# Attention scores of a one-token decode step: from one row per head to keys on the partitions, with the softmax divided out after the value product

## The chip, the cores and the metric

The kernel runs on one core of a Trainium2 chip. A core has a matrix engine (TensorE, PE in the profile, with its weight loads shown as PEld), a vector engine (VectorE, DVE), an activation engine (ScalarE, ACT), a general engine (GpSimd, POOL) and a queue engine (SyncE, SP) which here issues all transfers. The engines run side by side and wait for each other by semaphores. TensorE reads on-chip memory (SBUF) and writes the accumulator memory (PSUM), of which there are eight banks of 128 partitions by 512 fp32 values. The metric is the device time in microseconds; lower is better.

## The reference

One token of width 640 goes through an attention block and a feed-forward block, each behind a layer norm without weights and with a residual. Cut to what matters:

```python
q = (layernorm(x) @ wq)                   # 32 heads of 128
k = k_cache[:, :, 4096 - 1024:, :]        # the last 1024 of 4096 keys, 32 heads
v = v_cache[:, :, 4096 - 1024:, :]
p = softmax(q @ k^T * 128**-0.5)          # per head: 1024 scores
h = x + (p @ v) @ wo                      # wo: 4096 x 640
out = h + (gelu(layernorm(h) @ w_gate) * (layernorm(h) @ w_up)) @ w_down   # inner width 1728
```

All inputs are bf16. Every weight and every used key and value is read once, 33.9 MB together.

## The kernel before

The program is one list of instructions for each engine, written out by hand; the order in each list is the order of execution. `Wt(engine, tokens)` makes an engine wait for what `M(engine, token, instruction)` has marked. There is no planner.

SP issues the transfers in the order in which they are needed (L203 to L228): x, five slices of wq, keys in eight groups of four heads, values in eight groups, wo in four quarters of eight heads, then w_gate, w_up and w_down in four pieces. wo lies over wq and so waits for the last use of wq (token "ps_q", L214); the feed-forward weights lie over the keys and wait for the last key transpose (L218).

TensorE works as follows.

- q (L277 to L282): 160 matmuls with one moving column each give q with its 128 dimensions on the partitions and one column for each head.
- Keys (L283 to L288): for each head, `pe_transpose_batch` (L245) turns eight 128x128 blocks of keys into one PSUM bank; there are four such banks in rotation. VectorE (20 heads) or ScalarE (12 heads) copies the bank to one of six slots of `kT_sb` (`evac_batch`, L349). Two heads later `pe_scores_batch` (L256) computes the scores. The stationary operand is a 128x32 block of `qmask` in which only the column of this head is filled, the moving operand the transposed keys, 512 at a time. Over 32 heads these matmuls accumulate into `psS`, 32 partitions (heads) by 1024 keys, in two banks.
- Softmax (L289 to L296, L382 to L393, L443 to L447): VectorE takes the maximum of each row of `psS` and makes a bias of it; ScalarE does one exponential over 32x1024 with the row sum; VectorE inverts the sum and puts it on a diagonal `diag_r`. Eight matmuls against this diagonal turn the probabilities to keys-on-partitions and divide by the sum in one go, and VectorE copies them to `e_sb`.
- Values (L298 to L304): 256 matmuls with one moving column, eight for each head, accumulate the head's output into a column of `ps_o`, which ScalarE copies to `oT_sb` (L449).
- Output projection (L309 to L315): for each head two matmuls, 512 and 128 wide, with the head's column as stationary operand.
- The second layer norm (L394 to L408, L450 to L453), then gate (L326), up (L333) and the elementwise GELU, and down (L340): 14 chunks of two matmuls, 512 and 128 wide.
- VectorE adds the residual and SP stores the row (L225 to L228).

The scale that ScalarE applies in the exponential (`scl`, L375) holds both 128**-0.5 and the first layer norm's inverse deviation, which is therefore not applied to q.

## Time and profile before

| | us |
|---|---|
| median of 6 runs | 101.83 (101.08 to 103.22) |
| the profiled execution, device time | 101.67 |
| its span, first to last instruction | 99.6 |
| TensorE matmuls busy | 71.7 (72%) |
| TensorE weight loads busy | 44.1 (44%) |
| VectorE busy | 23.4 (24%) |
| ScalarE busy | 20.5 (21%) |
| GpSimd busy | 2.3 (2%) |
| transfers, mean rate over the span | 341 GB/s, 33.9 MB |

In the profile the span is cut into 40 equal slices of 2.49 us; each digit is a busy share in tenths, where 9 is 90% or more. A row of the groups names the line, the engine, what is written and read, the shapes and the number of instructions, then busy time in total, mean ns of one, and the idle time before them with its cause. Matmuls overlap, so the mean of one is longer than the distance between two starts. The chain of waits is followed back from the last instruction: each piece is what released the next one. "issue" is time in which an engine waited for nothing that the profile shows. In the table of stretches a row has the stretch, its length, busy time and count of each engine, and at the end TensorE's granted clock as a share of full speed, the transfer share and GB/s.

### The profile page before, as it was taken

Reading aid. Unit: us, or ns where it says so; the run is one execution under the profiler, and the core shown is the slowest. Engines: PE = TensorE matmul, PEld = TensorE weight load, DVE = VectorE, ACT = ScalarE, POOL = GpSimd, SP = SyncE. Lnnn points to the kernel's source line nnn. Section 1 sums busy time; section 2 is a strip of 40 time slices with the busy share of each in tenths; the row PEclk is TensorE's granted clock in tenths of the full one; section 3 lists DMA queues with packets and bytes.
Section 4 is the critical chain, followed back from the end, with each engine's and each line's share of the span. In section 5 each row is a group of like instructions: output and inputs, shape, how many; then the busy total and the mean of one; then the engine's idle time right before and its main releaser. Section 6 shows DMA issues by size and latency. Waiting matters only on the chain.

```text
span 99.6 us, 2145 instructions
## 1 busy us (share of the span) xinstructions
PE 71.7 (72%) x990; PEld 44.1 (44%) x990; DVE 23.4 (24%) x52; ACT 20.5 (21%) x26; POOL 2.3 (2%) x12
## 2 busy tenths in 40 slices
PE   0110005999999999999999607990899971698990
PEld 0010005993554554455455106990444530694430
DVE  0500000053325533432552241000000028032003
ACT  5600000004351244435124464000000004200000
POOL 7100000000000000000000000000000000000000
PEclk9999999999999999999999998555559999655589
DMA  1899999999999999999999999999999999993000
GB/s 43 352 421 421 428 414 392 387 385 388 386 386 387 387 386 388 391 379 387 388 387 385 385 376 363 364 367 356 362 385 410 404 403 389 367 353 116 0 0 1
DMA packets 16443, 34.02 MB, mean 342 GB/s; under 512 B 498, under 2 KB 6324, under 8 KB 15796
## 3 DMA queue, kind: packets, MB, share of 16 engines
q1 hardware_dynamic: 16436, 33.90, 91.7%
q8 instruction: 7, 0.11, 0.5%
HBM read 33.90 MB, written 0.00 MB: 341 GB/s over the span
## 4 chain that ended last, share of the span: by engine, by line
PE 70%; DMA 13%; DVE 5%; ACT 4%; issue 3%; SPq 2%; DVEq 0%
PE psbank L253 19%; DMA wq_sb<-in_A_wq_dram 13%; PE psS L260 10%; PE psbank L311 9%; PE psbank L302 7%; PE psS L262 7%; PE psbank L343 5%; PE psS L280 4%; SPq L198 2%; PE psbank L313 2%; PE psbank L336 2%; PE psbank L329 2%; ACT E_sb L444 1%; ACT L453 1%; DVE mrow L383 1%
## 5 line engine op out<-in xcount | busy, mean ns | idle before, releaser
L253 PEld LDWEIGHTS psbank<-ident,K_sb 128*128 128x128 bf16 x256 | 15.5, 102 | 12.7 <-issue 12.7
L253 PE MATMUL psbank<-ident,K_sb 128*128 128x128 bf16 x256 | 20.7, 229 | 0.0
L358 ACT ACTIVATE kT_sb<-psbank 128x1024 bf16<-128x1024 bf16 x12 | 12.3, 1023 | 38.4 <-PE psbank L253 38.4
L356 DVE COPY kT_sb<-psbank 128x1024 bf16<-128x1024 bf16 x20 | 13.8, 692 | 20.0 <-PE psbank L253 20.0
L260 PE MATMUL psS<-kT_sb,qmask 128*32 128x512 bf16 x32 | 12.7, 396 | 0.1
L262 PE MATMUL psS<-kT_sb,qmask 128*32 128x512 bf16 x32 | 12.4, 387 | 0.0
L280 PE MATMUL psS<-xcT,wq_sb 128*128 128x1 bf16 x160 | 5.0, 166 | 9.7 <-DMA wq_sb<-in_A_wq_dram 9.7
L311 PE MATMUL psbank<-wq_sb,oT_sb 128*1 128x512 bf16 x32 | 11.0, 445 | 0.3 <-ACT oT_sb L449 0.3
L280 PEld LDWEIGHTS psS<-xcT,wq_sb 128*128 128x128 bf16 x160 | 4.7, 104 | 10.1 <-DMA wq_sb<-in_A_wq_dram 9.5
L302 PE MATMUL psbank<-e_sb,V_sb 128*128 128x1 bf16 x256 | 7.1, 165 | 2.8 <-issue 2.3
L302 PEld LDWEIGHTS psbank<-e_sb,V_sb 128*128 128x128 bf16 x256 | 6.9, 103 | 3.0 <-issue 2.3
L313 PE MATMUL psbank<-wq_sb,oT_sb 128*1 128x128 bf16 x32 | 7.7, 242 | 0.0
L343 PE MATMUL psbank<-K_sb,aT 128*1 128x512 bf16 (+1 forms) x14 | 6.3, 534 | 0.4 <-DVE aT L426 0.4
L311 PEld LDWEIGHTS psbank<-wq_sb,oT_sb 128*1 128x1 bf16 x32 | 3.0, 94 | 5.9 <-issue 2.6
L395 DVE TENSOR_TENSOR h_rowf<-psbank,x_row 1x512 f32<-1x512 f32 x1 | 0.7, 679 | 20.8 <-PE psbank L313 20.8
L260 PEld LDWEIGHTS psS<-kT_sb,qmask 128*32 128x32 bf16 x32 | 3.0, 93 | 4.0 <-ACT kT_sb L358 0.6
L345 PE MATMUL psbank<-K_sb,aT 128*1 128x128 bf16 (+1 forms) x14 | 3.8, 271 | 0.0
L378 DVE CAST qmask<-psS 128x32 bf16<-128x32 f32 x1 | 0.3, 301 | 14.6 <-PE psS L280 14.6
L343 PEld LDWEIGHTS psbank<-K_sb,aT 128*1 128x1 bf16 (+1 forms) x14 | 1.5, 107 | 3.9 <-issue 3.0
L262 PEld LDWEIGHTS psS<-kT_sb,qmask 128*32 128x32 bf16 x32 | 3.1, 96 | 0.1
L270 PE MATMUL psS<-ones_bf,xc_row 1*128 1x1 bf16 x5 | 0.3, 160 | 3.9 <-DVE psbank L371 3.9
L313 PEld LDWEIGHTS psbank<-wq_sb,oT_sb 128*1 128x1 bf16 x32 | 3.0, 94 | 0.0
(70 smaller groups left out, 33.2 us busy)
## 6 DMA issues: line engine op xcount, KB each, us to landing
K_sb<-in_A_k_cache_dram SPq DMA_DIRECT2D x8, 1024.0 KB, 15.8
V_sb<-in_A_v_cache_dram SPq DMA_DIRECT2D x8, 1024.0 KB, 14.3
wq_sb<-in_A_wq_dram SPq DMA_DIRECT2D x5, 1024.0 KB, 8.9
wq_sb<-in_A_wo_dram SPq DMA_DIRECT2D x4, 1280.0 KB, 14.9
K_sb<-in_B_w_gate_dram SPq DMA_DIRECT2D x1, 2160.0 KB, 16.3
K_sb<-in_B_w_up_dram SPq DMA_DIRECT2D x1, 2160.0 KB, 17.7
K_sb<-in_B_w_down_dram SPq DMA_DIRECT2D x2, 640.0 KB, 14.5
K_sb<-in_B_w_down_dram SPq DMA_DIRECT2D x1, 800.0 KB, 17.7
```

The source lines that it names most:

```text
L198: sp.dma_start(out=out_ap, in_=in_ap).then_inc(sem, 16)
L253: t = pe.transpose(psT[bank][:, kk * 128:(kk + 1) * 128], K_sb[:, h, kk, :], ident[:, :])
L260: pe.matmul(psS0, lhsT=qmask[:, h * H:(h + 1) * H], rhs=kT_sb[:, slot, 0:512], start=(h == 0), stop=(h == H - 1))
L262: t = pe.matmul(psS1, lhsT=qmask[:, h * H:(h + 1) * H], rhs=kT_sb[:, slot, 512:1024], start=(h == 0), stop=(h == H - 1))
L280: t = pe.matmul(ps_q[:, h:h + 1], lhsT=wq_sb[:, c, h * DH:(h + 1) * DH], rhs=xcT[:, c:c + 1], start=(c == 0), stop=(c == DC - 1))
L302: t = pe.matmul(ps_o[:, h:h + 1], lhsT=V_sb[:, h, kk, :], rhs=e_sb[:, col:col + 1], start=(kk == 0), stop=(kk == KK - 1))
L311: pe.matmul(psA0, lhsT=oT_sb[:, h:h + 1], rhs=wo_view[:, h, 0:512], start=(h == 0), stop=(h == H - 1))
L313: t = pe.matmul(psA1, lhsT=oT_sb[:, h:h + 1], rhs=wo_view[:, h, 512:D], start=(h == 0), stop=(h == H - 1))
L343: pe.matmul(psD0, lhsT=aT[0:m, fc:fc + 1], rhs=wd_view[0:m, fc, 0:512], start=(fc == 0), stop=(fc == FC - 1))
L345: t = pe.matmul(psD1, lhsT=aT[0:m, fc:fc + 1], rhs=wd_view[0:m, fc, 512:D], start=(fc == 0), stop=(fc == FC - 1))
L356: ins = eng.tensor_copy(out=kT_sb[:, slot, :], in_=psT[bank][:, :])
L358: ins = eng.activation(out=kT_sb[:, slot, :], in_=psT[bank][:, :], func=ACT.Copy)
```

## The change

The scores are computed with the roles of the operands exchanged. For each head, eight matmuls have a 128x128 block of the transposed keys as stationary operand and the head's q, one column of the new `qT_sb`, as the moving one. Each writes one column of `ps_s`: 128 keys on the partitions, 256 columns for 32 heads by eight blocks. Nothing accumulates over heads, and `qmask` with its fill is gone. ScalarE, not VectorE, copies q from PSUM, ahead of its first key copy.

The softmax is then done in this layout. VectorE takes the maximum of each head over its eight columns (128x32), TensorE transposes that (`psM`), VectorE takes the maximum over the 128 partitions, puts it on a diagonal, and a matmul with ones spreads it to all partitions (`psMB`). VectorE copies it, subtracts it from the scores, and ScalarE does one exponential over 128x256, which gives the operand of the value product directly. A matmul with ones sums over the partitions (`psE`, 128x256); VectorE sums the eight columns of each head and inverts. This last is not needed before the end of the value product: its result is multiplied by the inverse when it leaves PSUM, on VectorE in place of ScalarE's copy.

The number of TensorE matmuls for the scores goes from 64 to 256; the eight matmuls against the diagonal go, and three single ones come.

```diff
@@ layout of PSUM
-        psS0 = psS[0:H, 0:512]
-        psS1 = psS[0:H, 512:1024]
-        psE = psb[0][:, 0:KK * H]
+        SOFF = 64
+        MBOFF = 64
+        ps5 = psS[:, 512:1024]
+        ps_s = ps4[:, SOFF:SOFF + H * KK]
+        ps_s3 = ps_s.rearrange("p (h kk) -> p h kk", kk=KK)
+        psM = ps5.bitcast(BF16)[0:H, 0:128]
+        psE = ps5[:, 0:H * KK]
+        psMB = psb[6][:, MBOFF:MBOFF + H]
@@ prog_pool
-            pool.memset(qmask[:, :], 0.0)
@@ pe_scores_batch
-            Wt("pe", ("E", b), "qmask")
-            pe.matmul(psS0, lhsT=qmask[:, h * H:(h + 1) * H], rhs=kT_sb[:, slot, 0:512],
-                      start=(h == 0), stop=(h == H - 1))
-            t = pe.matmul(psS1, lhsT=qmask[:, h * H:(h + 1) * H], rhs=kT_sb[:, slot, 512:1024],
-                          start=(h == 0), stop=(h == H - 1))
+            Wt("pe", ("E", b), "qT")
+            t = None
+            for kk in range(KK):
+                col = h * KK + kk
+                t = pe.matmul(ps_s[:, col:col + 1], lhsT=kT_sb[:, slot, kk * 128:(kk + 1) * 128],
+                              rhs=qT_sb[:, h:h + 1], start=True, stop=True)
@@ prog_pe
-            M("pe", "ps_r1", pe.matmul(ps_r1[0:H, :], lhsT=ones_f[0:1, 0:H], rhs=mv[0:1, 3:4],
+            M("pe", "ps_r1", pe.matmul(ps_r1[:, :], lhsT=ones_f[0:1, 0:128], rhs=mv[0:1, 3:4],
...
-            Wt("pe", "E", "diag_r", ("E", n_batches - NB))
-            for bb in range(n_batches - NB, n_batches):
-                if bb % NB == 0:
-                    Wt("pe", ("E", bb))
-            for kk in range(KK):
-                t = pe.matmul(psE[:, kk * H:(kk + 1) * H], lhsT=E_sb[0:H, kk * 128:(kk + 1) * 128],
-                              rhs=diag_r[0:H, 0:H], start=True, stop=True)
-            M("pe", "psE", t)
-            Wt("pe", "e_sb")
+            Wt("pe", "m1")
+            M("pe", "psM", pe.transpose(psM, m1_bf[:, :], ident[:, :]))
+            Wt("pe", "diag")
+            M("pe", "psMB", pe.matmul(psMB, lhsT=ones_bf[0:H, 0:128], rhs=diag[0:H, 0:H],
+                                         start=True, stop=True))
+            Wt("pe", "e", "m2")
+            M("pe", "psE", pe.matmul(psE, lhsT=ones_bf[:, :], rhs=e_bf[:, :], start=True, stop=True))
+            Wt("pe", "mbs")
             for h in range(H):
                 Wt("pe", ("V", h // 4))
                 for kk in range(KK):
-                    col = kk * H + h
-                    t = pe.matmul(ps_o[:, h:h + 1], lhsT=V_sb[:, h, kk, :], rhs=e_sb[:, col:col + 1],
+                    col = h * KK + kk
+                    t = pe.matmul(ps_o[:, h:h + 1], lhsT=V_sb[:, h, kk, :], rhs=e_bf[:, col:col + 1],
                                   start=(kk == 0), stop=(kk == KK - 1))
@@ prog_dve
-            Wt("dve", "ps_q")
-            M("dve", "qmask", dve.tensor_copy(out=qmask_diag, in_=ps_q))
...
             Wt("dve", ("S", n_batches - 1))
-            M("dve", "mrow", dve.tensor_reduce(out=mrow[0:H, :], in_=psS[0:H, :], axis=AX.X, op=ALU.max))
-            Wt("dve", "mrow", "scl")
-            M("dve", "nb", dve.scalar_tensor_tensor(out=nb[0:H, :], in0=mrow[0:H, :], scalar=-1.0, in1=scl[0:H, :],
-                                                    op0=ALU.mult, op1=ALU.mult))
-            Wt("dve", "E")
-            M("dve", "rinv", dve.reciprocal(out=rinv[0:H, :], in_=se[0:H, :]))
-            Wt("dve", "rinv", "ident")
-            M("dve", "diag_r", dve.tensor_scalar(out=diag_r[0:H, 0:H], in0=ident[0:H, 0:H],
-                                                 scalar1=rinv[0:H, 0:1], scalar2=None, op0=ALU.mult))
+            M("dve", "m1", dve.tensor_reduce(out=m1_bf[:, :], in_=ps_s3, axis=AX.X, op=ALU.max))
+            Wt("dve", "psM")
+            M("dve", "m2", dve.tensor_reduce(out=m2[0:H, 0:1], in_=psM, axis=AX.X, op=ALU.max))
+            Wt("dve", "m2", "ident")
+            M("dve", "diag", dve.tensor_scalar(out=diag[0:H, 0:H], in0=ident[0:H, 0:H],
+                                               scalar1=m2[0:H, 0:1], scalar2=None, op0=ALU.mult))
+            Wt("dve", "psMB")
+            M("dve", "mbs", dve.tensor_copy(out=mbs[:, :], in_=psMB))
+            Wt("dve", "mbs")
+            mb3 = bass.AP(tensor=mbs[:, :].tensor, offset=mbs[:, :].offset,
+                          ap=[list(mbs[:, :].ap[0]), [1, H], [0, KK]])
+            M("dve", "sm", dve.tensor_tensor(out=sm[:, :].rearrange("p (h kk) -> p h kk", kk=KK),
+                                             in0=ps_s3, in1=mb3, op=ALU.subtract))
             Wt("dve", "psE")
-            M("dve", "e_sb", dve.tensor_copy(out=e_sb[:, :], in_=psE))
+            M("dve", "rs", dve.tensor_reduce(out=rs[:, :], in_=psE.rearrange("p (h kk) -> p h kk", kk=KK),
+                                             axis=AX.X, op=ALU.add))
+            Wt("dve", "rs")
+            M("dve", "rinv", dve.reciprocal(out=rinv[:, :], in_=rs[:, :]))
+            Wt("dve", "ps_o", "rinv")
+            M("dve", "oT", dve.tensor_tensor(out=oT_sb[:, :], in0=ps_o, in1=rinv[:, :], op=ALU.mult))
@@ prog_act
+            Wt("act", "ps_q")
+            M("act", "qT", act.activation(out=qT_sb[:, :], in_=ps_q, func=ACT.Copy))
...
-            Wt("act", "nb", ("S", n_batches - 1))
-            M("act", "E", act.activation(out=E_sb[0:H, :], in_=psS[0:H, :], func=ACT.Exp,
-                                         bias=nb[0:H, 0:1], scale=scl[0:H, 0:1], accum_out=se[0:H, 0:1]))
-            Wt("act", "E")
+            Wt("act", "sm", "scl")
+            M("act", "e", act.activation(out=e_bf[:, :], in_=sm[:, :], func=ACT.Exp, scale=scl[:, 0:1]))
+            Wt("act", "e")
             M("act", "ln_warm2", act.activation(out=dummy[:, 2:3], in_=dummy[:, 0:1], func=ACT.Ln))
-            Wt("act", "ps_o")
-            M("act", "oT", act.activation(out=oT_sb[:, :], in_=ps_o, func=ACT.Copy))
```

## The prediction

> **What bounds the kernel now.** The page's slices come first, for the limit of each stage.

> ```profile
> PE   0110005999999999999999607990899971698990
> ...
> DMA  1899999999999999999999999999999999993000
> GB/s 43 352 421 421 428 414 392 387 385 388 386 386 387 387 386 388 391 379 387 388 387 385 385 376 363 364 367 356 362 385 410 404 403 389 367 353 116 0 0 1
> ```

> Both TensorE and the transfers look full from 15 us to 90 us. The transfers are one unbroken stream, so landings follow from the rates. Adding up the GB/s of one-microsecond stretches, wq is in at 15.1, K plus V (16.8 MB at 387 GB/s) at 58.5, wo (5.24 MB at about 364) at 72.9, wu at 84.0, wd at 90.5. The first user of wq started at 15.96, so I add 0.8 us from last byte to use: V's last group 59.3, wo's first quarter 62.9 and last 73.75, wu 84.8, wd 91.3. In before each is used later (V from 60.8, wo from 70.4, up from 88.1), so TensorE carries the chain. From the chain of waits, around the softmax (start, length):

> ```profile
> 56.61 1.22 DVE mrow L383
> ...
> 58.03 1.30 ACT E_sb L444 x2
> ...
> 60.29 0.44 DVE e_sb L393
> 60.73 0.05 issue
> 60.78 6.47 PE psbank L302 x238
> 67.24 2.27 issue
> 69.51 0.66 PE psbank L302 x18
> ```

> Softmax takes 4.2 us (56.58 to 60.78); then 256 one-column matmuls at 6.47/238 = 27.2 ns, with a 2.27 us hole that no engine or landing explains. The groups give the two kinds of K work:

> ```profile
> L253 PE MATMUL psbank<-ident,K_sb 128*128 128x128 bf16 x256 | 20.7, 229 | 0.0
> ...
> L356 DVE COPY kT_sb<-psbank 128x1024 bf16<-128x1024 bf16 x20 | 13.8, 692 | 20.0 <-PE psbank L253 20.0
> L260 PE MATMUL psS<-kT_sb,qmask 128*32 128x512 bf16 x32 | 12.7, 396 | 0.1
> ...
> L358 ACT ACTIVATE kT_sb<-psbank 128x1024 bf16<-128x1024 bf16 x12 | 12.3, 1023 | 38.4 <-PE psbank L253 38.4
> ...
> L302 PE MATMUL psbank<-e_sb,V_sb 128*128 128x1 bf16 x256 | 7.1, 165 | 2.8 <-issue 2.3 <-DVE e_sb L393 0.5
> ```

> Each row ends with busy time, mean ns of one, idle before it and the releaser: the copies wait for TensorE, not it for them. In the chain a head costs 0.55 (transposes) + 0.32 + 0.22 (two score matmuls) = 1.09 us. Last, the clock, in one-microsecond stretches (the third number from the end is the granted clock):

> ```profile
> 61.00:62.00 1.00, 1.00 (x45) 1.00 (x42) 0.00 (x0) 0.00 (x0) 0.00 (x0) 0.64 1.08 364
> ...
> 74.00:75.00 1.00, 1.00 (x5) 0.47 (x4) 0.00 (x0) 0.00 (x0) 0.00 (x0) 0.53 1.03 399
> ...
> 85.00:86.00 1.00, 0.57 (x4) 0.56 (x5) 0.00 (x0) 0.36 (x2) 0.00 (x0) 0.59 1.06 369
> ...
> 95.00:96.00 1.00, 1.00 (x8) 0.44 (x7) 0.00 (x0) 0.00 (x0) 0.00 (x0) 0.79 0.00 0
> ```

> Mixing 1.00 and 0.50, the clock falls at 61.28, rises at 74.94, falls at 85.18, rises at 95.42: apart by 13.66, 10.24 and 10.24, that is 4, 3 and 3 times 3.41. So it is decided on a fixed grid of 3.41 us. The row's 1.00 near 20 us is not to be trusted: the first 24 transposes took 2.58 us (107 ns each), later ones start 57 ns apart, and the change lies at 23.7, again on the grid.

> **The change, part by part.**

> *Score matmuls.* Two 512-wide ones (0.54 us) become eight one-column ones of the L302 shape: 8 x 27.2 ns = 0.22. A change of kind costs about 0.09: a second score matmul starts at 24.54 and the next head's transposes at 24.85, 0.31 later, of which 0.22 is the matmul's own stream; the change from transposes to scores is inside the 0.55. A head is then 0.55 + 0.22 + 0.09 = 0.86 us. Bounds: 0.77 (no switch cost) to 0.95 (twice).

> This rests on the clock staying full. [...] In the window 20.32 to 23.74, which opened it, wide matmuls filled only 0.95 us (28%), transposes nearly the rest. The windows 68.11 to 71.52 and 88.59 to 92.00 held 1.08 and 1.22 us of wide matmuls (32 and 36%) and did not open it. So transposes must count. Once open, streaming is 8 x 53 ns in 0.86, half the time, and the window 54.46 to 57.87 kept the gate open at 49% (seven transposes and six 512-wide matmuls, 1.67 us). I take 0.86.

> K then: start 20.1; three cold batches to 22.7, first scores and the fourth batch with the rise at 23.74, second scores, to 24.15; 28 heads x 0.86 = 24.1, to 48.25; the last scores wait for ScalarE's copy (1.02 plus hops), as now: 49.5, against 56.58. The copies still fit (VectorE 5 x 0.75 of 8 x 0.86 us).

> *Softmax.* Removed: the 4.2 us. Added on the path: maximum over 128x256 in PSUM 0.42 (as L393's CAST of that size), transpose and hop 0.32 (L318's five small matmuls take 0.30 from start to the next engine, L294's eight with the hop 0.52), second maximum over 128 columns 0.28 (L383's 1024 took 1.21, 1.04 ns a column beyond the 256 at 0.42), diagonal 0.22 (L390), broadcast matmul and hop 0.32, copy of 32 columns 0.20 (L408's one column 0.16, L378's 32 strided 0.30), subtraction 0.42 (L395's 512 took 0.68), exponential 0.38 (between L449's 32 columns at 0.20 and L358's 1024 at 1.02), sum matmul ahead of V 0.40: 2.96, with remaining hops 3.2. Bounds 2.8 to 4.2: nine small steps with a semaphore each. V starts at 52.7. On TensorE V stands behind the waits for "e" and "mbs"; nothing else is there to do. The row sums and reciprocal (0.7 us of VectorE) lie beside the V loop, 7 us, and cost nothing while it lasts; alone they would cost that 0.7. The scaling at the end replaces ScalarE's copy, 0.2 for 0.2.

> *V loop.* 6.96 us of matmuls, and the hole. [...] I take it inside V: oT at 62.3, and wo's first quarter lands at 62.9 either way.

> *After V nothing is edited, but landings now hold.* A head of wo takes 0.53 us at half clock (71.13 to 71.66 in the chain) and 0.27 at full. From 62.9 with the rise at 68.11, 24 heads are done at 72.0; the last quarter lands at 73.75, eight heads 2.18, result 76.15 against 81.5. From there to the gate matmuls 4.42 as now: 80.6, done 82.75. Up waits for wu at 84.8: 87.0, and 0.48 more: down starts at 87.5, against 90.78. So of 8.1 us gained at V's start 3.3 survive. Down in before had 4.64 us cold, 6.3 in all. By the same grid the clock rises at 92.0: 8.4 chunks x 0.533 + 5.6 x 0.272 = 6.0, end 93.5, against 97.1. Gain 3.6.

> *At nothing:* the removed qmask fill (0.95 on GpSimd) and the wider scale matmul lie under the wait for wq until 15.96; qT's copy (0.2) under the first transposes. GpSimd moves no data. SP's wait for the last transpose ends earlier, but its queue is full: wg was issued only at 64.2, long after 54.8. Without these covers they would cost 0.95, 0.1 and 0.2.

> Sum: profiled execution 101.67 us (span 99.6 and 2.07 around it) - 3.6 = 98.1. It stands 0.16 under the median 101.83, so 98.1 does for that too.

> **The rivals.**

> *A, forecast, 98.1 (62%).* Down may warm early (4.65 us, then 96.7) or never (7.46, then 99.5).

> *B, slower: the gate stays shut in K (15%).* [...]

> *C, a fetch hole on the path (13%).* More instructions, and a 2.27 us hole in gate, up or down instead of V: 100.4. [...]

> *D, landings later than I count, or half clock to the end (8%).* Completion 2 us behind the last byte instead of 0.8, and a cold down: 98.1 + 1.2 + 1.4 = 100.7. This is the case in which the edit does all it says and the transfer stream, unchanged at 33.9 MB to 90.5 us, takes almost all of it.

> Under 2%: better than A.

> **How the numbers follow.** A, C and D lie between 96.5 and 101.0 and make 83%; B is left out. A measurement of this kernel tells about 1% from no change (below 100.8, above 102.8): faster 0.78 (A, most of C, half of D), same 0.07, slower 0.15.

> **What would show it.** Right: heads 0.86 us apart from 24 us on; V starting near 52.7; TensorE waiting on wo and wu landings; gate beginning near 80.6; transfers ending at 90.5 as now. Wrong: transposes at 107 ns throughout (B); an unexplained TensorE pause after 80 us (C); V late because the nine softmax steps take over 5 us; a transfer stream that ends later than 90.5.

## The result, and the profile after

The changed kernel takes 99.38 us (median of 10 runs, 99.16 to 100.12) against 101.79 us (median of 20 runs, 100.78 to 103.22): a ratio of 0.980, 95% interval 0.977 to 0.983. Some executions of the kernel before fall into a slower state and its median moves with their number, so every ratio here is of fast runs alone. Run again among the experiments, the changed kernel took 99.31 beside a kernel before of 102.14, ratio 0.977 (0.971 to 0.983). The forecast was 98.1 with a range of 96.5 to 101.0: right in sign and in the limits that take over, 1.3 us too low, and of the 3.6 us that it promised 2.4 came. The profiled execution took 99.68 us, its span is 97.7 us.

The chain of waits of the changed kernel, around the opening of the clock and around the softmax (start, length, what):

```profile
24.11 0.88 PE psbank L255 x8
24.98 0.19 PE psS L265 x8
25.17 0.65 PE psbank L255 x8
25.82 0.18 PE psS L265 x8
26.00 0.47 PE psbank L255 x8
26.46 0.18 PE psS L265 x8
...
35.41 1.10 issue
...
41.84 0.86 issue
...
46.42 0.43 DVE m_bf L383
...
48.66 0.52 ACT e_bf L455
...
49.23 0.35 PE psS L298
```

A head at full clock takes 0.47 + 0.18 = 0.65 us where it took 1.09. The eight transposes go from 0.88 to 0.47 us, the change lying in the middle of one batch, and no wide matmul is left in this stage. Two holes for which the chain names no releaser ("issue"), 1.10 and 0.86 us, now lie here instead of in the value product. From the start of the first maximum to the sum matmul are 2.81 us.

What waited for transfers, in the list of waits (engine, line, releaser, total, times, longest):

```profile
PE psbank L304 <- DMA V_sb<-in_A_v_cache_dram: 4.7, 3, 1.7
PE psbank L313 <- DMA wq_sb<-in_A_wo_dram: 3.9, 2, 2.7
PE psbank L338 <- DMA K_sb<-in_B_w_up_dram: 1.9, 1, 1.9
```

None of the three was in the kernel before. The timeline of TensorE shows where the waits end (start, length, line, what, and in brackets the idle time before it):

```profile
49.35 4.45 PE L304 MATMUL psbank<-e_bf,V_sb 128*128 128x1 bf16 x160
...
60.78 1.01 PE L304 MATMUL psbank<-e_bf,V_sb 128*128 128x1 bf16 x32 [1.71 <-DMA V_sb<-in_A_v_cache_dram]
...
64.46 0.59 PE L313 MATMUL psbank<-wq_sb,oT_sb 128*1 128x512 bf16 x1 [2.67 <-DMA wq_sb<-in_A_wo_dram]
...
75.20 0.38 PE L313 MATMUL psbank<-wq_sb,oT_sb 128*1 128x512 bf16 x1 [1.26 <-DMA wq_sb<-in_A_wo_dram]
...
86.15 2.25 PE L338 MATMUL psbank<-hcT,K_sb 128*128 128x1 bf16 x70 [1.90 <-DMA K_sb<-in_B_w_up_dram]
```

The last three value groups, the first and the last quarter of wo, and w_up each hold TensorE up. In the kernel before, up had begun at 88.12:

```profile
88.12 2.25 PE L336 MATMUL psbank<-hcT,K_sb 128*128 128x1 bf16 x70
```

The value product began at 49.35 us, 11.4 us earlier than before; up began at 86.15, 2.0 us earlier. So 9.4 us are lost again between the two. The waits for landings take more than that, 10.5 us in sum; the hole of 2.27 us that is gone from the value product pays part of it. Down then ran from 88.79 to 95.2, at half clock until 93.7 (the granted clock is the third number from the end):

```profile
92.00:93.00 1.00, 1.00 (x6) 0.40 (x4) 0.00 (x0) 0.00 (x0) 0.00 (x0) 0.50 0.06 20
...
93.00:94.00 1.00, 1.00 (x7) 0.48 (x6) 0.00 (x0) 0.00 (x0) 0.00 (x0) 0.65 0.01 3
```

### The profile page after: what moved, and what is told of

Read it like the earlier page. It is cut to its first block, busy times and chain, and to the rows that moved or that the text cites. A ratio compares the mean times of both kernels' runs of the same rounds, so it can differ in the third digit from the quotient of the medians.

```text
span 97.7 us, 2519 instructions
## 1 busy us (share of the span) xinstructions
PE 61.1 (63%) x1177; PEld 49.0 (50%) x1177; DVE 23.3 (24%) x54; ACT 19.7 (20%) x25; POOL 1.4 (1%) x11
## 3 DMA queue, kind: packets, MB, share of 16 engines
q1 hardware_dynamic: 16436, 33.90, 93.7%
## 4 chain that ended last, share of the span: by engine, by line
PE 38%; DMA 31%; SPq 21%; issue 3%; DVE 3%; ACT 2%; DVEq 0%
SPq L201 21%; DMA K_sb<-in_B_w_up_dram 18%; PE psbank L255 18%; DMA wq_sb<-in_A_wq_dram 13%; PE psS L265 6%; PE psbank L345 5%; PE psS L283 4%; PE psbank L338 2%; PE psbank L347 1%; ACT kT_sb L360 1%; DVE out_row L438 1%; ACT e_bf L455 1%; DVE sm L394 0%; DVE m_bf L383 0%; PE psS L298 0%
## 5 line engine op out<-in xcount | busy, mean ns | idle before, releaser
L255 PE MATMUL psbank<-ident,K_sb 128*128 128x128 bf16 x256 | 21.6, 234 | 2.0 <-issue 2.0
L358 DVE COPY kT_sb<-psbank 128x1024 bf16<-128x1024 bf16 x20 | 13.7, 692 | 25.5 <-PE psbank L255 25.5
L255 PEld LDWEIGHTS psbank<-ident,K_sb 128*128 128x128 bf16 x256 | 16.6, 105 | 2.2 <-issue 2.2
L360 ACT ACTIVATE kT_sb<-psbank 128x1024 bf16<-128x1024 bf16 x12 | 12.3, 1024 | 13.2 <-PE psbank L255 13.2
L313 PE MATMUL psbank<-wq_sb,oT_sb 128*1 128x512 bf16 x32 | 11.6, 458 | 4.0 <-DMA wq_sb<-in_A_wo_dram 3.9
L265 PE MATMUL psS<-qT_sb,kT_sb 128*128 128x1 bf16 x256 | 11.1, 164 | 0.6 <-ACT kT_sb L360 0.6
L304 PE MATMUL psbank<-e_bf,V_sb 128*128 128x1 bf16 x256 | 7.7, 166 | 4.8 <-DMA V_sb<-in_A_v_cache_dram 4.7
L265 PEld LDWEIGHTS psS<-qT_sb,kT_sb 128*128 128x128 bf16 x256 | 9.7, 98 | 0.8 <-ACT kT_sb L360 0.7
L304 PEld LDWEIGHTS psbank<-e_bf,V_sb 128*128 128x128 bf16 x256 | 7.3, 104 | 5.1 <-DMA V_sb<-in_A_v_cache_dram 4.9
L338 PE MATMUL psbank<-hcT,K_sb 128*128 128x1 bf16 (+1 forms) x70 | 2.2, 167 | 1.9 <-DMA K_sb<-in_B_w_up_dram 1.9
L338 PEld LDWEIGHTS psbank<-hcT,K_sb 128*128 128x128 bf16 (+1 forms) x70 | 2.1, 107 | 2.0 <-DMA K_sb<-in_B_w_up_dram 2.0
```

The costliest lines, as they stand in the source:

```text
L255: t = pe.transpose(psT[bank][:, kk * 128:(kk + 1) * 128], K_sb[:, h, kk, :], ident[:, :])
L265: t = pe.matmul(ps_s[:, col:col + 1], lhsT=kT_sb[:, slot, kk * 128:(kk + 1) * 128], rhs=qT_sb[:, h:h + 1], start=True, stop=True)
L304: t = pe.matmul(ps_o[:, h:h + 1], lhsT=V_sb[:, h, kk, :], rhs=e_bf[:, col:col + 1], start=(kk == 0), stop=(kk == KK - 1))
L313: pe.matmul(psA0, lhsT=oT_sb[:, h:h + 1], rhs=wo_view[:, h, 0:512], start=(h == 0), stop=(h == H - 1))
L338: t = pe.matmul(ps_u[0:m, fc:fc + 1], lhsT=wu_view[:, c, fc * 128:fc * 128 + m], rhs=hcT[:, c:c + 1], start=(c == 0), stop=(c == DC - 1))
L358: ins = eng.tensor_copy(out=kT_sb[:, slot, :], in_=psT[bank][:, :])
```

## The experiments

Every kernel below is the changed one with an edit, except where it says the kernel before. The median of the kernel before moved between 101.8 and 102.9 from one comparison to the next. The changed kernel itself ran in two of the four, with 99.38 and 99.31; times are set against these, and a difference of a few tenths of a microsecond says nothing. In the code, "..." stands for what is left out.

### How much of the earlier start counts

A chain of useless VectorE copies holds the value product back:

```diff
@@ prog_pe, ahead of the value product
             Wt("pe", "mbs")
+            Wt("pe", "stall")
...
@@ prog_dve, after rinv
+            for i in range(14):                       # 9, 14 or 22
+                M("dve", ..., dve.tensor_copy(out=kT_sb[:, 0, :], in_=psT[0][:, :]))
+                Wt("dve", ...)
```

With 14 copies:

> The changed kernel with 14 useless VectorE copies of 128x1024 (0.69 us each) between the sum matmul and the value product, on which TensorE waits: the value product starts at about 60.7 us instead of 49.4, as late as in the kernel before. Theory F (the end is set by the landing of w_up, at 86.15; what TensorE wins before it is slack): no change against the changed kernel, 99.4 us, at most +0.3. Rival G (TensorE's chain still sets the end, and the earlier start is what was gained): as slow as the kernel before, 101.8, +2.4.

With 22:

> The same with 22 copies: the value product starts at about 66.5. Theory F: the slack is used up by now, the output projection begins near 73.8 at half clock and the up matmuls come some 5 us later than the landing: +5 (4 to 6), about 104.5. Rival G: +8, about 107.5.

And with 9, run after those two:

> The changed kernel with 9 useless VectorE copies ahead of the value product, which starts near 57.1 us instead of 49.4. Theory F3 (TensorE has about 9.8 us of slack at that place, read from the run with 14 copies: 11.3 us later there came out 1.5 us later at up): no change, 99.4 us within 0.3. Rival G2 (the gain is proportional to the earlier start, 1.5 us for 11.3): +1.0, 100.4.

| copies | value product starts | up starts | time | against the kernel before |
|---|---|---|---|---|
| 0 | 49.4 | 86.1 | 99.31 to 99.38 | 0.977 and 0.980 |
| 9 | 57.0 | 86.0 | 99.06 | 0.971 (0.965 to 0.977) |
| 14 | 60.7 | 87.6 | 100.86 | 0.995 (0.988 to 1.001) |
| 22 | 66.6 | 93.1 | 106.68 | 1.051 (1.035 to 1.066) |

TensorE's timeline with 9 copies:

```profile
56.95 4.91 PE L305 MATMUL psbank<-e_bf,V_sb 128*128 128x1 bf16 x179 [7.30 <-DVE kT_sb L404]
64.02 2.21 PE L305 MATMUL psbank<-e_bf,V_sb 128*128 128x1 bf16 x77 [2.16 <-issue]
...
86.03 2.25 PE L339 MATMUL psbank<-hcT,K_sb 128*128 128x1 bf16 x70 [1.71 <-DMA K_sb<-in_B_w_up_dram]
```

With 14 copies:

```profile
60.70 4.91 PE L305 MATMUL psbank<-e_bf,V_sb 128*128 128x1 bf16 x179 [10.92 <-DVE kT_sb L404]
67.77 2.21 PE L305 MATMUL psbank<-e_bf,V_sb 128*128 128x1 bf16 x77 [2.16 <-issue]
...
87.64 2.25 PE L339 MATMUL psbank<-hcT,K_sb 128*128 128x1 bf16 x70
```

With 22 copies:

```profile
66.58 4.92 PE L305 MATMUL psbank<-e_bf,V_sb 128*128 128x1 bf16 x179 [16.72 <-DVE kT_sb L404]
73.66 2.21 PE L305 MATMUL psbank<-e_bf,V_sb 128*128 128x1 bf16 x77 [2.16 <-issue]
...
93.08 2.25 PE L339 MATMUL psbank<-hcT,K_sb 128*128 128x1 bf16 x70
```

7.6 us of delay cost nothing: up still waits for w_up. With 14 copies it no longer waits. Beyond some 10 us each microsecond counts whole: from 14 to 22 copies the start moves by 5.9 us and the time by 5.8. So of the 11.4 us won at the value product only the last 1.5 or so reach the end. With 14 copies the value product starts as late as in the kernel before, and what is left against that kernel is not clear of noise (0.995, 0.988 to 1.001): the earlier start is most of the gain. Theory F holds in kind, but its allowance of 0.3 us at 14 copies was missed by 1.2, and 22 copies cost 7.3, not 5: F had left out that the hole of 2.16 us comes back into the value product as soon as landings no longer pace it. With 9, 14 and 22 copies it comes after the same 179 matmuls and ends at 64, 68 and 74 us. It belongs to the instruction stream, not to the time.

### The deferral alone

```diff
@@ prog_dve, after rinv; shortened: en_bf3, e_bf3 and ri3 are views by head; the value product takes en_bf and waits for it
+            M("dve", "en", dve.tensor_tensor(out=en_bf3, in0=e_bf3, in1=ri3, op=ALU.mult))
...
-            M("dve", "oT", dve.tensor_tensor(out=oT_sb[:, :], in0=ps_o, in1=rinv[:, :], op=ALU.mult))
+            M("dve", "oT", dve.tensor_copy(out=oT_sb[:, :], in_=ps_o))
```

> The changed kernel without the deferral: the row sums, the reciprocal and a multiplication of the probabilities come before the value product, which starts some 1.3 us later; the output of the value product is only copied. Theory F: no change, 99.4 us within 0.3, since the value product waits for its landings at 53 to 61 us anyway. Rival H (the deferral is part of the gain): +1.3, 100.7.

99.38 us (99.17 to 99.67). The value product started at 51.42 instead of 49.35 and ended on the same last group:

```profile
60.70 1.01 PE L306 MATMUL psbank<-en_bf,V_sb 128*128 128x1 bf16 x32 [0.85 <-DMA V_sb<-in_A_v_cache_dram]
```

The deferral puts 2.1 us of work aside and gains nothing here; rival H is out. Even a hole of 2.16 us that appeared in this value product, again after 179 matmuls, cost nothing: the last group was still waited for.

### The tail: clock, landings and instruction blocks

Useless wide matmuls in TensorE's gaps are meant to keep the clock up:

```diff
+        def keep_warm(pe, n):
+            for i in range(n):
+                pe.matmul(psb[3][:, 0:512], lhsT=ident[:, :], rhs=kT_sb[:, 0, 0:512], start=True, stop=True)
@@ prog_pe: 12 after ps_attn, 4 after ps_hcT, one in every second gate chunk, 5 ahead of up, 1 ahead of down
```

> The changed kernel with 29 useless 512-wide matmuls in TensorE's gaps between the output projection and the down matmuls (12 before the second layer norm's transposes, 4 after, one in every second gate chunk, 5 ahead of up, 1 ahead of down), so that the clock gate sees work. Theory F: up still starts with the landing of w_up near 86.1, but the 14 chunks of down run at full clock (0.27 us instead of 0.53) up to the last landings near 92.7 us: 1.6 us faster, 97.8. Rival (the last landing sets the end, whatever the clock): no change, 99.4. If the useless matmuls only lengthen the path: slower, 100 or more.

99.46 us (99.16 to 100.71): no gain that can be told; the 97.8 expected was missed. The clock fell at 88.7 and rose at 92.1, so the first half of down was still at half clock; and the chain of waits now ends on w_down:

```profile
78.99 14.06 DMA K_sb<-in_B_w_down_dram
93.09 0.38 PE psbank L355
```

The third piece of w_down landed at 93.05, later than the 92.7 expected of the last landings, and five chunks followed it. In the changed kernel the down matmuls, at half clock, reach that piece only near 93 as well: two limits lie on the same spot, and lifting one shows nothing. Which of them ends last changes from one execution to the next. In the profile above, the clock rose at 93.70 and no wait for w_down stands in the chain. In the second profile of the same kernel (99.18 us) the clock rose at 92.30, and the chain ends on that piece, which landed at 93.09 (start and length of its transfer):

```profile
78.92 14.17 DMA K_sb<-in_B_w_down_dram
```

The same wide matmuls in the kernel before:

> The kernel before, scores and softmax untouched, with the 29 useless 512-wide matmuls between output projection and down. Theory F2 (the tail is bound by two things that nearly coincide: half clock in down and the last landings near 92 us): down starts at 90.8 as before and the clock is full for at least half of it: 1.2 to 2.5 us faster than the kernel before, about the time of the changed kernel, though no score or softmax is touched. Rival (only an earlier start of the value product gains): no change.

101.52 us (100.78 to 102.98) against 102.14, ratio 0.999 (0.994 to 1.003): no change, and the expectation missed. Down ran at full clock throughout (93.33 to 97.4 instead of 90.8 to 97.1), but it began 2.5 us later, because there no landing makes TensorE wait between gate and down, and the twelve wide matmuls in gate and ahead of up lie on the path (12 x 0.22 us). The clock is bought there at its own price.

Up on halves of w_up:

```diff
-            dma(sp, "wu", wu_view, ...)
+            dma(sp, ("wu", 0), wu_view[:, :, 0:896], ...)
+            dma(sp, ("wu", 1), wu_view[:, :, 896:F], ...)
```

> The changed kernel with w_up moved in two halves of columns, so that up starts on the first half some 2.8 us earlier. Theory F2: down starts 1.1 us earlier, near 87.7, its first nine chunks gain that, but the last five still wait for the landing near 93: 0.3 to 0.6 us faster. Rival (the landing of w_up alone sets the end): 1.1 us faster.

99.64 us against 99.31: no gain, and the expectation of 0.3 to 0.6 us missed. Up was cleared earlier, but now down waits for its own pieces:

```profile
88.69 0.59 PE L347 MATMUL psbank<-K_sb,aT 128*1 128x512 bf16 x1 [1.04 <-DMA K_sb<-in_B_w_down_dram]
```

Up and down each have a landing right behind them. The rival, that w_up alone sets the end, is out.

What sets those landings? The trace holds sixteen landing signals for each transfer, as many as the 16 engines that the page counts for the core. In the changed kernel half of the signals for the last value group are in by 59.04, the last at 60.73; the matmuls wait for the last. It also holds 16 KB packets of kind "instruction". The trace names no engine for them; each is taken here as the fetch of one block of TensorE's instructions. Between the starts of the first and the last packet TensorE starts 1557 matmuls and weight loads in the kernel before, 260 to a packet, and 1954 in the changed one, 244 to a packet; "half a block" and "a third of a block" in two of the texts below stand for 128 and 84 of such instructions. There are seven packets before and nine after (packets, MB, share):

```profile
q8 instruction: 7, 0.11, 0.5%
...
q8 instruction: 9, 0.15, 0.6%
```

Set beside each other, signals and packets tell more. In the changed kernel the sixteen signals of a transfer lie within 0.35 us up to the landing at 21.3. The first instruction packet runs from 21.20 to 22.25, and from the next landing on one signal comes 1.6 us behind the other fifteen. With each further packet one more signal is late by some 1.5 us, up to eight behind the eighth packet (75.4). In the kernel before, six are late behind six packets. The ninth packet ran from 90.29 to 91.34. Behind it the count stays at eight, but one signal is 3.3 us behind the first: for the third piece of w_down fifteen signals were in by 91.70 and the sixteenth came at 93.44. In the kernel before, whose seventh and last packet began at 89.95, that piece's sixteenth came at 91.72. To move the packets, TensorE got 64 useless one-column matmuls ahead of q, with the wide matmuls also in up (the "fourth last piece" in the text below is the third of the four):

```diff
+            for i in range(64):
+                pe.matmul(psb[3][:, 0:1], lhsT=ones_bf[:, :], rhs=ones_bf[:, 0:1], start=True, stop=True)
```

> The changed kernel with the useless wide matmuls also in up (one after every third chunk), and 64 useless one-column matmuls while TensorE waits for wq, which shift where TensorE's instruction blocks end by half a block. Theory L (a fetch of a TensorE instruction block near 90 us sits in one transfer engine's queue and makes the fourth last piece of w_down land 1.4 us later, at 93.1 to 93.4 instead of 91.8): with the fetch moved away that piece lands near 91.8, down runs at full clock from its start near 89.6: 1.4 to 1.9 us faster than the changed kernel, about 97.7. Rival (the last landing is 93 us whatever the instruction stream): 0 to 0.4 us faster.

99.76 us (99.24 to 100.86): expectation missed. The ninth packet did move, to 85.3, but that is worse: the first piece of w_down came at 89.53 (fifteen signals by 88.31) instead of 88.36, and down waited for it; the third came still at 93.05. The late landing moved with the packet, which speaks for the link. So does the first packet: here it ran from 19.79 to 20.90, and the landing whose signals were still together at 21.3 in the changed kernel now has its last signal at 22.67, 1.2 us behind the other fifteen. But a packet out of the way was not reached. So instructions were taken away instead. The last six heads (ten in the second kernel) get one score matmul with eight wrong columns in place of eight matmuls; the rest of their scores is left out:

```diff
@@ pe_scores_batch
+            if h >= H - 6:                            # 10 in the second kernel
+                t = pe.matmul(ps_s[:, h * KK:(h + 1) * KK], lhsT=kT_sb[:, slot, 0:128],
+                              rhs=qT_sb[:, 0:KK], start=True, stop=True)
+                M("pe", ("S", b), t)
+                return
...
```

> The changed kernel in which the last six heads get one score matmul with eight wrong columns instead of eight matmuls: 42 matmuls with their weight loads less, so that part of the scores is left out and TensorE's instruction blocks end a third of a block later. Theory L (an instruction fetch in the tail makes the transfers behind it land late): the fetch now at 90.3 us comes after down or falls away, and the last landings come near 91.9 instead of 93.2; the time stays within 0.3 of 99.4, because down at half clock reaches that piece only near 93. Rival (the last landing has nothing to do with instructions): it stays at 93.2, 99.4 us.

99.54 us (99.02 to 100.04), no change, as expected. The ninth packet came only at 91.4; the third piece landed at 91.82 and the last at 92.15, and down waited for none of them. Together with the wide matmuls:

> The same with ten heads cut (70 matmuls with their loads less; their scores are left out) and the 29 useless wide matmuls in the tail. Theory L with F2: last landings near 91.9 us and down at full clock from about 92 at the latest: 0.8 to 1.2 us faster than the changed kernel, about 98.4. Rival: as the run with the wide matmuls alone, 99.4.

97.95 us (97.84 to 99.13), ratio to the kernel before 0.961 (0.953 to 0.968): 1.4 us below the changed kernel, and 1.6 below the shortened kernel of the same comparison. In its chain of waits the same transfer ends at 91.8, where it ended at 93.05 in the run with the wide matmuls alone:

```profile
79.12 12.67 DMA K_sb<-in_B_w_down_dram
```

The clock was full from 69.4 to the end of down. So the tail is bound by both: either limit lifted alone left 99.5, both together gave 1.4 us less. (In the run with the wide matmuls alone the clock was not full throughout either, but there the landing came last.) The cut also shortens the score stage, but the runs with a delayed value product show that a start some microseconds earlier or later changes nothing. No run here takes so many TensorE instructions away and still computes every score.

## Why the prediction was right, and where it was off

- **Which limit follows.** Right. The forecast said that value groups, wo and w_up would hold TensorE, and all three do. That the transfers would not change is right up to w_up: they carry 33.9 MB, and w_up's last byte by the summed rates is at 84.2 us (84.0 before). It is wrong for the end: the third piece of w_down landed 1.7 us later than before (93.44 against 91.72). The forecast had no term for that.
- **The clock in the key stage.** Right. From 25.4 us on the granted clock was full, transposes started 55 to 56 ns apart (106 to 107 before; the forecast's 53 is half of that), and only transposes and one-column matmuls had been running. One-column matmuls alone had not raised it in the kernel before: 224 of them from 61.30 to 68.10 us stand at a granted clock of 0.50 throughout. Rival B is out: the clock rose, and a head cost 0.65 us.
- **A head at 0.86 us.** Too dear by 0.21: the 0.09 for a change of kind did not come, the transposes took 0.47 instead of the 0.55 that they took between 512-wide matmuls, and the scores 0.18 instead of 0.22. 0.21 x 28 = 5.9 us less, of which the two holes of 1.96 us and the later rise of the clock took back part; the value product started at 49.4, not 52.7. With some 9.8 us of slack (11.3 us of delay with 14 copies brought up 1.5 us later) this had no effect.
- **Softmax at 3.2 us.** Nearly right: last score matmul to value product took about 3.0.
- **The fetch hole in the value product.** Wrong place, without effect. That the hole of 2.27 us is a fetch, and that it would stay in the value product, was the author's estimate. Two holes lie in the key stage; held back, the value product shows one again. That they are waits for instruction blocks is not shown, but the times speak for it: each ends 1.3 to 1.5 us behind the end of an instruction packet, those of the key stage (36.51 behind 34.98, 42.70 behind 41.43), that of the kernel before (69.51 behind 68.16) and those with 9, 14 and 22 copies. That the product of the last group still came near the forecast, 62.0 us against 62.3, is luck: the hole was missing and the last value group landed 1.4 us late.
- **From last byte to use, 0.8 us.** This is the step that made the forecast too low. It was taken from wq, the first transfer, which landed before any instruction packet. Use came 2.0 us behind the summed bytes for the last value group (60.78 against 58.74), 2.0 for wo's last quarter (75.20 against 73.17) and 1.9 for w_up (86.15 against 84.23). Up began at 86.15 instead of the forecast's 84.8, and down at 88.79 instead of 87.5: 1.3 us. Rival D had this at 2 us, as an unlikely case. The profile of the kernel before already held the right number. Its timeline of issues and its table of landings put w_up, issued at 68.23 and landing 17.7 us later, at 85.9 us, where the summed bytes and 0.8 us gave 84.8:

```profile
68.23 2.20 SPq L198 DMA_DIRECT2D K_sb<-in_B_w_up_dram  x1
...
K_sb<-in_B_w_up_dram SPq DMA_DIRECT2D x1, 2160.0 KB, 17.7
```

- **Down, 6.0 us.** It took 6.4, with the rise at 93.7 instead of 92.0: 0.4 us. The two terms add to 1.7 us, against 99.68 - 98.1 = 1.6 in the profiled execution. The second term varies: in the changed kernel, too, the clock changes (at 25.43, 49.33, 69.81, 80.05, 93.70 and 97.11 us) lie 7, 6, 3, 4 and 1 times 3.41 us apart, but the forecast took the phase from the profile of the kernel before, and in the second profile of the changed kernel the rise came at 92.3 and the landing of w_down at 93.1 held the down matmuls instead; they took 6.2 us in all.
- **Rival C**, a fetch hole in gate, up or down, did not happen. What did happen was not foreseen: the ninth packet, from 90.29 to 91.34 us, did not stop TensorE, which began a chunk of down every 0.53 us throughout, but behind it the third piece of w_down landed at 93.44, 1.7 us after its fifteenth signal.

## What to carry to other kernels

When one engine is the chain and a full transfer stream runs beside it, a stage made 10 us faster is worth only its distance to the next landing (here 11.4 us at the value product became 2.0 at up); take the landings from the profile's issue times and times to landing, or, if you sum the rates, the delay from last byte to use from late in the stream, not from its first transfer. Where the tail has two limits on the same spot, here half clock and the last landing, a test that lifts one shows nothing, and only both together tell. And count instructions: 192 more score matmuls with their weight loads were cheap on TensorE, but with them nine 16 KB instruction packets stood in the transfer stream instead of seven, and in the profiled execution its last landings came 1.7 us later.
